# A retention layer and a wave MLP on one core: q loaded in 1024-byte rows, a half of the partitions at a time, in a new order of work

## The chip, the cores and the metric

One core of a Trainium2 chip runs the whole kernel. The metric is device time in microseconds (us) of one execution; the time given is the median of the runs. An engine is PE (matrix), DVE (vector), ACT (scalar) or POOL; SP only issues DMAs. ACT and POOL issue DMAs too.

## The reference

The inputs are q, k and v of shape (4, 8, 768, 64) (batch, head, token, dimension), and four weights. Cut to what matters:

```python
for t in range(S):                                   # retention, scale = 1/8
    state = gamma[h] * state + outer(k[t], v[t])     # gamma[h] = 1 - 2**(-5-h)
    y[t] = scale * q[t] @ state
x = y as (batch, token, 512)
theta = x @ w_theta
y = w_tok_r @ (x * cos(theta)) + w_tok_i @ (x * sin(theta))   # over tokens
u = x + y
out = u + maximum(u @ w_ch, 0)                       # float32 (4, 768, 512)
```

## The kernel before, in words

**Units and chunks.** The attention is cut into 24 units. Unit n is 256 tokens of four heads: n % 2 is the half of the heads, n // 2 the block of 256 tokens, three blocks to a batch. A chunk C is 128 tokens of all 512 columns, 24 in all, six to a batch. Two units (2i and 2i + 1) make chunks 2i and 2i + 1.

**The order is written out by hand.** `ORDER` is a list of tokens; each calls the function of its name with its arguments, and the last letter may name the engine or the queue (`a` ACT, `v` DVE, `p` POOL, `s` SP). Each engine and each queue works through its own tokens in that order. The steps:

| token | what it does | engine |
|---|---|---|
| Lq, Lk, Lv n | load q, k or v of unit n, 256 KB float32, two tokens to a partition, rows of 512 bytes | SP or ACT queue |
| ck, cq, cqs, cv n | cast k, cast q, or scale q by its decay, scale v; to bf16 (tiles kqb, vb) | letter |
| Tk, Tq, E n or Dk n | transpose k and q: on PE (tile kq_ps) with a copy E to kqT, or by a DMA transpose on SP | PE + letter, or SP |
| A, m n | k times q (at_ps), then the causal mask (at) | PE, DVE |
| ST, S0, S1, SB n | k times v, the state's running sum, its copy to bf16 (sbd) | PE, DVE or letter |
| I, Y n | state times q and at times v, into r_ps | PE |
| XA or XB n.c | r_ps to xT; XA multiplies by the decay table qx, XB copies where cqs scaled q already | DVE, letter |
| Tx, Ex C or Dx C | transpose xT to x, by PE and a copy or by a DMA transpose | PE + letter, or SP |
| Hh, CN C, z C | theta (th_ps), its sine and cosine, times x | PE, ACT, letter |
| Pth, Pch, Pw r.g | load w_theta (wth), w_ch (wch), a group of rows of w_tok_r or w_tok_i; float32 in HBM, cast to bf16 on the way | POOL queue |
| Tw, Ew r.t | transpose a block of w_tok | PE, letter |
| M t.s, u t | one of six token blocks of chunk t's y (y_ps), both weights; then u = x + y | PE, DVE |
| Tu, Eu t or Du t | transpose u, by PE and a copy or by a DMA transpose | PE + letter, or SP |
| O, f, SO t | u times w_ch (o_ps); maximum and sum (tile ot, 4 buffers); store of 256 KB | PE, DVE, SP or ACT queue |
| Mh, uh, Tuh, Euh, Oh, fh, SOh | the same for the last chunk in two column halves, with stores of 128 KB | as above |
| Z | two matmuls of zeros of 512 columns (tile zz) | PE |

The const tokens make tables: const1 zeros and tiles, const2 positions and log decays, const3 the decays qsc (for cqs) and vsc (for cv), constA positions along tokens, const8 and const9 the table qx for the first 256 and the other 512 tokens, const4 the identity, const5 the causal mask, const6 zeroes sbd, const7 a first sine.

M needs z of all six chunks of a batch, and so all six units of it.

Of the kernel before, what the change touches and what calls it, by code (L numbers as in the profile page):

```python
# [15 lines left out]
FT = mybir.dt.float32  # L16
# [6 lines left out]
const2 Lv.0.s const1 const6.v Z.29 Z.2 const5 Z.38 Lk.0.a const3 Z.35 Z.8 Lq.0.s Lv.1.s Z.28 constA  # L23
const4 Lq.1.a cqs.0.v const9 Lk.1.s cv.0.p Z.39 const8 ck.0.p Tk.0 Tq.0 ck.1.a E.0.v Lq.4.a ST.0
Lk.4.a Z.15 A.0 cqs.1.p Tq.1 Lq.2.s S0.0.v SB.0.1.v Lk.2.s SB.0.0.p cv.1.p Lv.2.s S1.0 I.0 Z.27 m.0
Tk.1 E.1.a Y.0 ST.1 XB.0.1.a cqs.2.v Z.34 S0.1.v S1.1 cv.2.p SB.1.0.a Pth Lq.3.s Z.18 XB.0.0.v Tq.2
A.1 SB.1.1.a ck.2.a Tk.2 const7 I.1 Z.23 m.1 Y.1 XB.1.0.a Lk.3.s E.2.v XB.1.1.v A.2 ck.3.p m.2 ST.2
# [54 lines left out]
M.22.0 M.21.5 M.22.3 M.22.5 Du.19 M.21.4 SO.17.s M.22.4 Du.18 M.21.0 O.19 Mh.1.0 Mh.1.2 M.21.3
M.20.2 Mh.1.4 u.22 O.18 f.19 M.20.0 M.20.1 Tuh.0 u.21 Du.22 Du.21 f.18 M.20.3 Euh.0 M.20.4 Mh.1.1
M.20.5 u.20 O.22 Mh.1.5 uh.1 f.22 Tu.20 SO.14.a SO.19.s Eu.20.a O.21 SO.18.a Tuh.1 Euh.1 f.21 O.20
f.20 Oh.0 Oh.1 SO.21.a SO.22.s SO.20.s fh.1 SOh.1 fh.0 SOh.0 Z.31
# [14 lines left out]
def kernel(  # L100
# [64 lines left out]

    def Lq(n, e):
        load_unit("qf", q, n, e)
# [35 lines left out]
    def const2():  # L203
        posn = const.tile([P, nI, 2], FT, name="posn")
# [9 lines left out]
        K["zerob"] = const.tile([P, 1], FT, name="zerob")  # L214
        nc.gpsimd.memset(K["zerob"], 0.0)
# [78 lines left out]
    def ck(n, e):  # L294
        copy(e, in_blocks(kqb_of(n)[:, 0]), by_token(raw["kf", n]))
# [338 lines left out]
```

## Time and profile before

| what | before |
|---|---|
| median of 3 runs | 169.24 us (168.81, 169.24, 169.62) |
| the profiled execution's own time | 168.7 us |
| its span | 166.9 us |
| busy: PE, DVE, ACT, POOL | 153.7, 114.0, 78.7, 76.6 us |
| DMA packets, bytes | 69,062, 34.93 MB |
| one load of q, from issue to landing, median | 5.0 us on SP's queue, 5.4 us on ACT's |

The span runs from the first to the last record of the profiled execution; the time of that execution lies 1.8 us above it. The page's slices cut the span into 40 equal parts of 4.17 us, and a digit is a busy share in tenths. The DMA share is the sum over the 16 DMA engines of the time that packets took; it can exceed 1 in the table of stretches, since packets of one engine overlap. Line numbers are those of the kernel before.

### The profile page before, as it was taken

What the parts mean: (1) busy time and instruction counts of PE and PEld (TensorE: products, weight loads), DVE (VectorE), ACT (ScalarE), POOL (GpSimd) and SP (SyncE); (2) the same over time, 40 slices, a digit from 0 to 9 for tenths busy, and PEclk for the clock granted to TensorE, in tenths of its full rate; (3) what the DMA queues carried; (4) which work ended last, traced back from release to release, by engine and by line L of the source; (5) the groups of instructions that cost most, each with busy time, mean ns of one, the idle gap of its engine ahead of it and who ended that gap; (6) DMA issues with size and microseconds to landing.
All of it is one profiled execution on the core that took longest, in us unless ns stands there. A gap on an engine that the chain in (4) does not pass through costs nothing.

```text
span 166.9 us, 4887 instructions
## 1 busy us (share of the span) xinstructions
PE 153.7 (92%) x2001; PEld 86.8 (52%) x2030; DVE 114.0 (68%) x210; ACT 78.7 (47%) x141; POOL 76.6 (46%) x110
## 2 busy tenths in 40 slices
PE   5997779998999999999999999969999999999992
PEld 2455546655666556654555555435545544454550
DVE  3298657989994896994779895659868561254462
ACT  4965879981558345763333735822151426000020
POOL 7957369179206642630217699910459303600000
PEclk9999999999999999999999999999999999999999
DMA  4999999999999998949999995999899539414355
GB/s 121 297 290 244 280 282 265 259 227 251 195 197 224 296 184 203 312 102 266 298 301 191 173 245 146 260 215 232 150 216 162 119 64 247 159 61 127 88 211 208
DMA packets 69062, 34.93 MB, mean 209 GB/s; under 512 B 26416, under 2 KB 66096, under 8 KB 69040
## 3 DMA queue, kind: packets, MB, share of 16 engines
q1 hardware_dynamic: 56032, 23.73, 66.9%
q10 hardware_dynamic: 10320, 7.47, 15.5%
q0 software_dynamic: 2688, 3.41, 12.1%
q8 instruction: 16, 0.26, 0.7%
q14 instruction: 6, 0.05, 0.1%
HBM read 25.69 MB, written 6.29 MB: 192 GB/s over the span
## 4 chain that ended last, share of the span: by engine, by line
PE 75%; DMA 11%; ACT 5%; DVE 4%; issue 2%; POOL 2%; DVEq 0%; SPq 0%; POOLq 0%; ACTq 0%
PE y_ps L509 34%; PE o_ps L536 11%; PE th_ps L469 10%; DMA kqf<-in_k_dram 4%; PE r_ps L423 4%; DMA kqf<-in_q_dram 3%; DMA out_dram<-ot 3%; ACT qx L233 3%; PE at_ps L346 3%; PE w_ps L491 3%; PE r_ps L411 2%; PE kq_ps L316 2%; PE y_ps L561 2%; PE x_ps L455 1%; PE r_ps L373 1%
## 5 line engine op out<-in xcount | busy, mean ns | idle before, releaser
L509 PE MATMUL y_ps<-z,wtr 128*128 128x512 bf16 x131 | 49.8, 380 | 2.2 <-DVE ot L542 1.2
L509 PE MATMUL y_ps<-z,wti 128*128 128x512 bf16 x131 | 49.7, 379 | 1.0 <-issue 1.0
L483 POOL TENSOR_TENSOR z<-cs,x_sb 128x1024 bf16<-128x1024 bf16 x12 | 25.4, 2122 | 17.6 <-ACT cs L476 9.8
L355 DVE TENSOR_TENSOR at<-at_ps,mask 128x1024 bf16<-128x1024 f32 x24 | 29.2, 1216 | 0.6 <-PE at_ps L346 0.5
L308 POOL TENSOR_TENSOR vb<-vf,vsc 128x512 bf16<-128x512 f32 x18 | 18.8, 1047 | 21.3 <-DMA vf<-in_v_dram 20.9
L542 DVE SCALAR_TENSOR_TENSOR ot<-o_ps,u 128x512 f32<-128x512 f32 x23 | 15.9, 689 | 15.3 <-PE o_ps L536 12.1
L469 PE MATMUL th_ps<-wth,xT 128*128 128x512 bf16 x88 | 23.9, 380 | 0.5
L516 DVE TENSOR_TENSOR u<-y_ps,x_sb 128x512 bf16<-128x512 f32 x23 | 15.8, 688 | 11.5 <-PE y_ps L509 11.3
L536 PE MATMUL o_ps<-wch,uT 128*128 128x512 bf16 x88 | 23.2, 380 | 0.4 <-issue 0.2
L476 ACT ACTIVATE cs<-th_ps,zerob 128x512 bf16<-128x512 f32 x24 | 16.4, 685 | 13.0 <-PE th_ps L469 8.5
L476 ACT ACTIVATE cs<-th_ps,halfpi 128x512 bf16<-128x512 f32 x24 | 16.3, 685 | 12.9 <-issue 6.8
L139 POOL CAST sbd<-s 64x256 bf16<-64x256 f32 (+1 forms) x21 | 8.9, 423 | 26.9 <-DVE s L391 24.8
L509 PEld LDWEIGHTS <-wti 128*128 128x128 bf16 x138 | 13.5, 98 | 14.2 <-issue 2.5
L509 PEld LDWEIGHTS <-wtr 128*128 128x128 bf16 x138 | 13.4, 97 | 12.8
L137 ACT COPY kqT<-kq_ps 128x1024 bf16<-128x1024 bf16 x11 | 11.1, 1012 | 8.7 <-PE kq_ps L316 8.7
L137 ACT CAST kqb<-kqf 128x512 bf16<-128x512 f32 x17 | 10.3, 619 | 7.7 <-DMA kqf<-in_k_dram 6.0
L469 PEld LDWEIGHTS <-xT 128*128 128x128 bf16 x96 | 8.8, 98 | 8.3
L536 PEld LDWEIGHTS <-uT 128*128 128x128 bf16 x92 | 8.4, 98 | 8.6
L316 PE MATMUL kq_ps<-ident,kqb 128*128 128x128 bf16 x120 | 11.0, 220 | 0.5 <-ACT kqb L137 0.2
L278 PE MATMUL zz<-zero 128*128 128x512 bf16 x27 | 9.3, 477 | 2.0 <-DVE zero L192 1.9
L137 ACT CAST sbd<-s 64x256 bf16<-64x256 f32 (+1 forms) x19 | 6.9, 363 | 8.7 <-DVE s L139 4.0
L423 PE MATMUL r_ps<-at,vb 64*64 64x128 bf16 x384 | 10.0, 221 | 1.0 <-DVE at L355 1.0
(77 smaller groups left out, 207.0 us busy)
## 6 DMA issues: line engine op xcount, KB each, us to landing
vf<-in_v_dram SPq DMA_DIRECT2D x20, 256.0 KB, 5.8
kqf<-in_k_dram SPq DMA_DIRECT2D x19, 256.0 KB, 5.2
kqf<-in_q_dram SPq DMA_DIRECT2D x17, 256.0 KB, 5.0
out_dram<-ot ACTq DMA_DIRECT2D x12, 256.0 KB, 2.9
out_dram<-ot SPq DMA_DIRECT2D x11, 256.0 KB, 3.1
kqf<-in_q_dram ACTq DMA_DIRECT2D x7, 256.0 KB, 5.4
kqf<-in_k_dram ACTq DMA_DIRECT2D x5, 256.0 KB, 4.8
vf<-in_v_dram ACTq DMA_DIRECT2D x4, 256.0 KB, 5.3
```

The costliest lines, as they stand in the source:

```text
L137: nc.scalar.copy(dst, src)
L308: engines[e].tensor_mul(in_blocks(vb), by_token(raw["vf", n]), _bcast_last(K["vsc"][:, i, :, h * HU:(h + 1) * HU], D))
L316: nc.tensor.transpose(st["kq_ps", n][:, 4 * w + x, :], st["kqb", n][:, w, x * P:(x + 1) * P], K["ident"])
L355: nc.vector.tensor_mul(at.rearrange("p g j a t -> p (g j) (a t)"), st["at_ps", n].rearrange("p g j a t -> p (g j) (a t)"), _bcast_mid(K["m ...
L423: nc.tensor.matmul(st["R", n + 1][c][g * D:(g + 1) * D, j * P:(j + 1) * P], st["vb", n][rows, lo:lo + D], st["at", n][rows, g, j, a, :], s ...
L469: nc.tensor.matmul(th_ps, st["xT", C][:, j, :], K["wth"][:, j, :], start=(j == 0), stop=(j == 3))
L476: nc.scalar.activation(st["cs", C][:, w, :], st["th_ps", C], AF.Sin, bias=K["zerob" if w else "halfpi"], scale=1.0)
L483: engines[e].tensor_mul(st["z", b][:, c], st["cs", C], _bcast_mid(x_of(C), 2))
L509: nc.tensor.matmul(st["y", t], K["wT"][r][:, s0, t0 * P:(t0 + 1) * P], st["z", b][:, s0, r, :], start=(done == 0 and r == 0), stop=(done = ...
L516: nc.vector.tensor_add(st["u", t], st["y", t], st["x", b][:, t0, :])
L536: nc.tensor.matmul(o_ps, st["uT", t][:, j, :], K["wch"][:, j, :], start=(j == 0), stop=(j == nD - 1))
L542: nc.vector.scalar_tensor_tensor(st["ot", t], st["o", t], 0.0, st["u", t], ALU.max, ALU.add)
```

## The change

q is loaded by two DMAs a unit, Lq (partitions 0 to 63) and Lr (64 to 127), each 128 KB. A partition now holds four tokens of two heads in place of two tokens of four heads, so that a row in HBM is 1024 bytes. Everything that reads q follows: the scale table qsc has four tokens and two heads to a partition, cq and cqs put four token groups of 128 columns into kqb, A and I take 4 x 32 columns of the transposed q in place of 2 x 64, the mask and XA and XB have four tokens in place of two. k and v stay as they are. The table qx, which XA uses, is kept.

const2 now begins with the zero bias and a first Exp on ACT, and makes positions and log decays for q's new layout (two more position fills on POOL, eight small fills and one product on DVE).

The order is new throughout. In numbers of tokens: q loads 24 to 48 (Lq and Lr); loads issued by ACT 16 to 36 and by SP 56 to 60; Dk 9 to 10, Dx 12 to 11, Du 16 to 17; z on POOL 12 to 8; XB on ACT 17 to 10 and on DVE 9 to 16; Ew on ACT 3 to 8; SB on ACT 19 to 24; cv on POOL 18 to 15; Z 15 to 13. XA stays at 22, and M, Hh, O, A, Y, I and ST stay as they are in number.

```diff
+    def q_load(n, j, e):
+        b, i, h = unit(n)
+        if ("qf", n) not in raw:
+            raw["qf", n] = io.tile([P, 2, 4, D], FT, name="kqf", bufs=16)
+        queues[e].dma_start(
+            out=raw["qf", n][j * D:(j + 1) * D].rearrange("p g a d -> p g (a d)"),
+            in_=q[b, h * HU:(h + 1) * HU, i * 2 * P:(i + 1) * 2 * P, :].rearrange(
+                "(j g) (p a) d -> j p g (a d)", g=2, a=4)[j])
     def Lq(n, e):
-        load_unit("qf", q, n, e)
+        q_load(n, 0, e)
+    def Lr(n, e):
+        q_load(n, 1, e)
...
     def const2():
+        K["zerob"] = const.tile([P, 1], FT, name="zerob")
+        nc.gpsimd.memset(K["zerob"], 0.0)
+        nc.scalar.activation(const.tile([P, 1], FT, name="warm"), K["zerob"], AF.Exp,
+                             bias=K["zerob"], scale=1.0)
...
+    def q_by_token(ap):
+        return ap.rearrange("p g a d -> p a g d")
+    def q_blocks(ap):
+        return ap.rearrange("p (a g d) -> p a g d", a=4, g=2)
+    def qT(n, rows, j, c):
+        lo = j * D + c * D // 2
+        return st["kqT", n][rows, 1].rearrange("p a j t -> p (a j) t")[:, :, lo:lo + D // 2]
...
     def cq(n, e):
-        copy(e, in_blocks(kqb_of(n)[:, 1]), by_token(raw["qf", n]))
+        copy(e, q_blocks(kqb_of(n)[:, 1]), q_by_token(raw["qf", n]))
...
-                                         kqT[rows, 1, :, j, cols],
+                                         qT(n, rows, j, c),
...
-        return (st["xT", C][:, 2 * h:2 * h + 2].rearrange("p j (t a) -> p j t a", a=2),
-                st["R", n + 1][c][:, :2 * P].rearrange("p (j a t) -> p j t a", j=2, a=2))
+        return (st["xT", C][:, 2 * h:2 * h + 2].rearrange("p j (t a) -> p j t a", a=4),
+                st["R", n + 1][c][:, :2 * P].rearrange("p (j a t) -> p j t a", j=2, a=4))
```

The order up to the first M, before and after:

```text
before
const2 Lv.0.s const1 const6.v Z.29 Z.2 const5 Z.38 Lk.0.a const3 Z.35 Z.8 Lq.0.s Lv.1.s Z.28 constA
const4 Lq.1.a cqs.0.v const9 Lk.1.s cv.0.p Z.39 const8 ck.0.p Tk.0 Tq.0 ck.1.a E.0.v Lq.4.a ST.0
Lk.4.a Z.15 A.0 cqs.1.p Tq.1 Lq.2.s S0.0.v SB.0.1.v Lk.2.s SB.0.0.p cv.1.p Lv.2.s S1.0 I.0 Z.27 m.0
Tk.1 E.1.a Y.0 ST.1 XB.0.1.a cqs.2.v Z.34 S0.1.v S1.1 cv.2.p SB.1.0.a Pth Lq.3.s Z.18 XB.0.0.v Tq.2
A.1 SB.1.1.a ck.2.a Tk.2 const7 I.1 Z.23 m.1 Y.1 XB.1.0.a Lk.3.s E.2.v XB.1.1.v A.2 ck.3.p m.2 ST.2
S0.2.v S1.2 SB.2.1.a Z.11 cqs.3.p Tq.3 Lv.3.s Tx.0 Tk.3 Z.3 ck.4.p Lv.4.s Lk.5.s Lq.5.s Lv.5.s
Lq.6.s Lk.6.s Lv.6.s Lq.7.s E.3.a SB.2.0.v I.2 Y.2 XB.2.1.a Ex.0.a cv.3.v cq.4.p Tk.4 Lq.8.s A.3
ST.3 Lk.7.s S0.3.v SB.3.0.a S1.3 Lv.7.s Lk.8.s Tx.1 Tq.4 SB.3.1.p cv.4.p m.3 Pw.1.0 XB.2.0.a Ex.1.a
I.3 Lv.8.s cq.5.a Y.3 E.4.a Pw.0.0 ST.4 Hh.0 ck.5.a cv.5.v CN.0.1 A.4 CN.0.0 S0.4.v Tq.5 Hh.1 Tk.5
XB.3.0.v SB.4.0.p XB.3.1.v SB.4.1.a Pw.0.1 Hh.2 m.4 E.5.v I.4 Y.4 ST.5 ck.6.a Tk.6 Tx.2 cq.6.a
CN.1.1 CN.1.0 XA.4.1 A.5 XA.4.0 m.5 Lq.9.s Ex.2.v S0.5.v z.0.p Tq.6 E.6.a CN.2.0 cv.6.p Hh.3
SB.5.0.v Tx.3 Tw.1.0 z.1.v SB.5.1.a Ew.1.0.v Ex.3.a CN.2.1 A.6 I.5 Y.5 ST.6 XA.5.0 z.2.v Tw.0.0
CN.3.0 Tx.4 CN.3.1 Ew.0.0.v S0.6.v XA.5.1 Ex.4.v Hh.4 CN.4.0 CN.4.1 Tw.0.1 M.0.1
...
M.20.5 u.20 O.22 Mh.1.5 uh.1 f.22 Tu.20 SO.14.a SO.19.s Eu.20.a O.21 SO.18.a Tuh.1 Euh.1 f.21 O.20
f.20 Oh.0 Oh.1 SO.21.a SO.22.s SO.20.s fh.1 SOh.1 fh.0 SOh.0 Z.31

after
const1 Z.40 Z.2 Z.10 const2 constA const4 Lv.0.a Lr.0.s Lr.1.s Lq.1.s Lq.0.a const5 const6.v const3
const8 Lk.0.s cq.0.a cq.1.a Z.43 Z.25 Lk.1.s ck.1.a cv.0.v ck.0.v ST.0 S0.0.v S1.0 Lk.2.s Lk.4.s
Tk.0 Tq.0 SB.0.1.a E.0.v Tk.1 Lv.1.s Lr.2.s ck.4.p cv.1.p ck.2.a SB.0.0.a I.0 A.0 Lq.2.s Lk.3.a Tq.1
Lq.3.s cqs.2.p Lr.4.s Z.18 Tk.2 Lq.4.s Lv.2.s E.1.a m.0 const9 Lr.3.a Z.37 Y.0 cq.3.a A.1 cqs.4.v
Tq.2 Tk.4 Z.17 ck.3.a Z.7 XA.0.0 E.2.v ST.1 cv.2.p Pth m.1 Lv.4.s Lk.5.s S0.1.v Lq.5.s SB.1.0.p
cv.4.p XA.0.1 A.2 S1.1 Tq.3 Tk.3 SB.1.1.a Lv.3.s I.1 Y.1 ST.2 Lr.5.s Lr.6.s m.2 XA.1.0 E.3.a Z.20
S0.2.v cq.5.a SB.2.1.a Lr.7.a Pw.0.0 S1.2 Tq.4 Tx.0 A.3 XA.1.1 Pw.0.1 Z.39 Lq.6.s SB.2.0.p I.2 E.4.a
cv.3.p Pw.1.0 cq.6.p Y.2 ST.3 Ex.0.v m.3 ck.5.a S0.3.v S1.3 XB.2.1.a A.4 SB.3.0.p Lv.5.s XB.2.0.v
Tx.1 Tq.5 SB.3.1.a Tk.5 Z.27 Lk.6.s Lv.6.s E.5.v I.3 Y.3 ST.4 XA.3.1 Z.0 XA.3.0 S0.4.v Tx.3 const7
cv.5.p SB.4.0.p Ex.3.a SB.4.1.a Lr.8.a Hh.0 Hh.1 Tx.2 Ex.1.v m.4 I.4 Y.4 ST.5 A.5 Tq.6 CN.0.1 Lk.7.a
CN.0.0 CN.1.1 CN.1.0 Ex.2.v Lk.8.a Lv.7.a z.0.v XB.4.1.a Hh.3 Tw.0.0 XB.4.0.v ck.6.p z.1.v Pw.1.1
S0.5.v SB.5.1.p Tk.6 Hh.2 CN.3.1 SB.5.0.p m.5 Ew.0.0.v Lq.8.a E.6.a I.5 Y.5 XA.5.1 Lv.9.a A.6 CN.3.0
Tw.0.2 CN.2.1 cv.6.p z.3.v Ew.0.2.a CN.2.0 Tw.1.0 Lr.9.a Hh.5 Ew.1.0.v Pw.1.2 CN.5.1 Pch XA.5.0
z.2.v Tw.0.1 Tx.5 Hh.4 ST.6 CN.5.0 Lq.7.s Ex.5.v z.5.v Ew.0.1.a Lv.8.s CN.4.0 CN.4.1 S0.6.a SB.6.1.p
Tx.4 M.0.0
...
M.20.3 M.20.2 Tuh.1 SO.18.a Euh.0 Euh.1 u.20 SO.15.s SO.19.s Du.22 O.22 Du.21 f.22 Tu.20 Eu.20.a
Oh.0 Oh.1 fh.0 fh.1 SO.22.a SOh.0 O.20 f.20 O.21 SO.20.s f.21 SO.21.s SOh.1
```

In the middle of the new order SO.7.s stands just ahead of A.19, M.12.1, M.12.2, M.12.5 and O.11, and f.11 behind them.

More of the change, by code (lines that the diff above doesn't have):

```diff
@@ L22 @@
 ORDER = """
[L23 to L27, printed above, removed]
@@ L82 @@
[L82 to L85, printed above, removed]
+const1 Z.40 Z.2 Z.10 const2 constA const4 Lv.0.a Lr.0.s Lr.1.s Lq.1.s Lq.0.a const5 const6.v const3
+const8 Lk.0.s cq.0.a cq.1.a Z.43 Z.25 Lk.1.s ck.1.a cv.0.v ck.0.v ST.0 S0.0.v S1.0 Lk.2.s Lk.4.s
@@ new lines @@
+Tk.0 Tq.0 SB.0.1.a E.0.v Tk.1 Lv.1.s Lr.2.s ck.4.p cv.1.p ck.2.a SB.0.0.a I.0 A.0 Lq.2.s Lk.3.a Tq.1
+Lq.3.s cqs.2.p Lr.4.s Z.18 Tk.2 Lq.4.s Lv.2.s E.1.a m.0 const9 Lr.3.a Z.37 Y.0 cq.3.a A.1 cqs.4.v
+Tq.2 Tk.4 Z.17 ck.3.a Z.7 XA.0.0 E.2.v ST.1 cv.2.p Pth m.1 Lv.4.s Lk.5.s S0.1.v Lq.5.s SB.1.0.p
+cv.4.p XA.0.1 A.2 S1.1 Tq.3 Tk.3 SB.1.1.a Lv.3.s I.1 Y.1 ST.2 Lr.5.s Lr.6.s m.2 XA.1.0 E.3.a Z.20
+S0.2.v cq.5.a SB.2.1.a Lr.7.a Pw.0.0 S1.2 Tq.4 Tx.0 A.3 XA.1.1 Pw.0.1 Z.39 Lq.6.s SB.2.0.p I.2 E.4.a
+cv.3.p Pw.1.0 cq.6.p Y.2 ST.3 Ex.0.v m.3 ck.5.a S0.3.v S1.3 XB.2.1.a A.4 SB.3.0.p Lv.5.s XB.2.0.v
@@ new lines @@
+z.2.v Tw.0.1 Tx.5 Hh.4 ST.6 CN.5.0 Lq.7.s Ex.5.v z.5.v Ew.0.1.a Lv.8.s CN.4.0 CN.4.1 S0.6.a SB.6.1.p
+Tx.4 M.0.0 M.0.2 Ex.4.v cqs.7.v z.4.v M.0.1 Tw.1.1 Pw.0.2 cv.7.p S1.6 ck.7.p M.0.5 cqs.8.p M.0.3
+M.0.4 Ew.1.1.a u.0 m.6 M.1.5 M.1.2 Lq.9.s Lk.9.s SB.6.0.a M.1.4 M.1.1 I.6 Tw.1.2 Ew.1.2.v Tk.7 Tq.7
+M.1.0 ck.8.a cv.8.v Tk.8 M.1.3 E.7.a Y.6 ST.7 XA.6.1 S0.7.v XA.6.0 A.7 m.7 S1.7 SB.7.0.p Tu.0 M.2.5
+M.2.1 Tq.8 SB.7.1.a Eu.0.a E.8.a M.2.4 M.2.3 Tw.1.4 Lr.11.s Lq.12.s Ew.1.4.a Lq.11.s I.7 M.2.0 A.8
@@ new lines @@
+Tq.15 f.5 cv.15.v Y.13 ST.14 M.8.1 M.8.4 Lv.20.s Lr.17.s u.9 XA.13.0 XA.13.1 cqs.16.v S0.14.v
+SB.14.0.p M.8.0 M.8.5 M.8.3 S1.14 Hh.13 E.15.a SO.3.a Lq.19.s Eu.6.a M.8.2 SB.14.1.v cv.20.v I.14
+Y.14 A.15 ST.15 Du.7 Lq.17.s u.8 XA.14.0 S0.15.v Lv.19.a CN.13.0 CN.13.1 Lk.19.a M.10.5 O.6 M.10.3
+S1.15 f.6 m.15 XA.14.1 cv.16.v SB.15.1.a ck.19.v M.10.4 M.10.2 Dk.18 Lk.21.a SB.15.0.p cqs.17.p
+cv.17.p cqs.19.p Hh.12 CN.12.1 Tx.13 M.10.0 M.10.1 Dk.16 Lr.21.a CN.12.0 Lv.18.s Ex.13.a I.15 Y.15
+ST.16 z.13.p A.16 O.7 u.10 Tx.12 Dk.17 XA.15.1 S0.16.v XA.15.0 f.7 Hh.15 M.11.5 Ex.12.a ck.20.a
@@ L213, in const2 @@
         nc.gpsimd.memset(K["halfpi"], math.pi / 2.0)
-        K["zerob"] = const.tile([P, 1], FT, name="zerob")
-        nc.gpsimd.memset(K["zerob"], 0.0)
+        posq = const.tile([P, nI, 4], FT, name="posq")
+        lgq = const.tile([P, 2, 2], FT, name="lgq")
+        for j in range(2):
+            rows = slice(j * D, (j + 1) * D)
+            nc.gpsimd.iota(posq[rows], pattern=[[2 * P, nI], [1, 4]], base=1, channel_multiplier=4,
+                           allow_small_or_imprecise_dtypes=True)
+            for h in range(2):
+                for g in range(2):
+                    nc.vector.memset(lgq[rows, h, g:g + 1], math.log(gammas[h * HU + 2 * j + g]))
+        argq = const.tile([P, nI * 4, 4], FT, name="argq")
+        nc.vector.tensor_mul(argq, _bcast_last(posq.rearrange("p i a -> p (i a)"), 4),
+                             _bcast_mid(lgq.rearrange("p h g -> p (h g)"), nI * 4))
+        K["argq"] = argq
         arg = const.tile([P, nI * 2, H], FT, name="arg")
@@ L266, in const5 @@
                     out=mask[rows, a], in_=mask[rows, a], compare_op=ALU.is_ge, fill=0.0,
-                    base=-a, pattern=[[1, 2], [2, D]], channel_multiplier=-2)
+                    base=-a, pattern=[[1, 4], [4, D // 2]], channel_multiplier=-2)
         K["mask"] = mask
```

118 lines of the change are left out of this document (55 added, 63 removed).

## The prediction

> **What bounds the kernel now.** I read the page first: the busy rows and the slices.
>
> ```profile
> PE 153.7 (92%) x2001; PEld 86.8 (52%) x2030; DVE 114.0 (68%) x210; ACT 78.7 (47%) x141; POOL 76.6 (46%) x110
> ...
> PE   5997779998999999999999999969999999999992
> ...
> DMA  4999999999999998949999995999899539414355
> ```
>
> PE is busy 92% of the span and the only engine near it; its weak slices are the first eight (to 33 us) and one at 109 us. DMA is full up to about 115 us. So there are two stages: one in which PE waits for data, and one in which it has a stock of work. The chain of waits over the first 30 us shows where they join.
>
> ```profile
> 9.25 6.63 DMA kqf<-in_k_dram
> ...
> 15.90 0.37 SPq L157
> ...
> 16.31 5.65 DMA kqf<-in_q_dram
> ...
> 22.04 0.62 ACT kqb L137
> 22.66 0.92 ACT kqT L137
> 23.59 0.04 issue
> 23.63 0.42 PE at_ps L346 x16
> ```
>
> Everything up to A.4 (23.63) hangs on two loads: k of unit 4 lands at 15.88, and only then SP issues Lk.5.s; q of unit 5 lands at 21.97, ACT does cq.5, then E.4, then PE does A.4. From there the chain is PE. The stretches tell how fast data comes, what outputs cost, and where PE still has holes.
>
> ```profile
> 6.00:9.00 3.00, 2.79 (x39) 1.25 (x41) 1.69 (x3) 3.00 (x7) 2.41 (x3) 1.00 1.22 290
> ...
> 108.00:111.00 3.00, 2.01 (x53) 1.01 (x53) 0.44 (x1) 1.44 (x4) 0.90 (x3) 1.00 1.34 202
> ...
> 162.00:164.00 2.00, 1.78 (x12) 0.97 (x10) 1.53 (x4) 0.00 (x0) 0.00 (x0) 1.00 0.83 303
> ```
>
> The columns are the stretch, its length, busy time of PE, PEld, DVE, ACT and POOL, PE's clock, the DMA share and GB/s. Loads in 512-byte rows move 290 GB/s at a share of 1.22, so 256 KB takes 0.90 us. The first two loads land near 5.1 us, and at 0.90 us each the fourteenth should land at 5.1 + 12 x 0.90 = 15.9: it does (15.88). The seventeenth (q of unit 5) should land at 18.6 and lands at 21.97; the 3.4 us between are wth, issued by POOL at 12.51: 1.05 MB of float32 at 290 GB/s is 3.6 us. The start is therefore bound by bytes. From 30 us to PE's last useful matmul (163.3) the stretches of 6 us leave PE idle only 4.5 us, 1.24 of it in the second row above, where DVE's f.11 waits for an output store:
>
> ```profile
> 110.56 0.69 DVE L542 SCALAR_TENSOR_TENSOR ot<-o_ps,u 128x512 f32<-128x512 f32 x1 [3.05 <-DMA out_dram<-ot]
> ```
>
> The end is 163.3 (last Oh), two halves of fh to 164.08, and a 128 KB store issued at 164.10; span 166.9, profiled run 168.7, so 1.8 us lie around the span. The median shown is 169.24, 0.54 above that run.
>
> **The change part by part.**
>
> *q's packets.* Six q units must land before A.4 in both orders, and 17 unit loads in all (v 0-4, k 0-5, q 0-5). A unit of q goes from 512 packets of 512 bytes to 256 of 1024. Upper end of the gain: outputs (2 KB rows) move 303 GB/s at share 0.83, 365 per unit of share against 290/1.22 = 238, so at equal share 256 KB takes 0.59 us. A straight line per packet between 1.77 ns (0.90 us / 512) and 4.6 ns (0.59 us / 128) gives 2.7 ns at 1024 bytes, 0.70 us a unit: 0.20 saved. Other end: no load of before writes only 64 partitions; if a half got half the rate, a unit would take 1.80 us, 0.90 lost. Size is nearest to the load rows, and the two changes pull apart, so I take a saving of 0.10 a unit, 0.6 us by A.4; ends -1.2 and +5.4.
>
> *POOL's weight loads.* Pth moves behind cv.2.p, that is behind v of unit 2, which has 12.5 units up to and with it: 5.1 + 10.5 x 0.90 = 14.5, plus 1.04 for cv.2: issue at 15.6 instead of 12.51. So part of wth falls behind q of unit 5. But Pw.0.0 and Pw.0.1 (0.39 and 0.79 MB of float32) follow cv.4.p on the same queue, near 17 instead of 21.9 and 24.2. With 1.05 MB landing 6.9 us after issue the POOL queue gets half to 0.6 of the rate; q of unit 5 then lands at L = 18.0 + 0.5 (L - 15.6) = 20.4, or 21.6 with 0.6 (the 0.6 us of q is in the 18.0). Against 21.97 that is -0.4 to -1.6 for both items; I take **-1.0**.
>
> *ACT ahead of A.4.* SB.2.1.a (0.40) and the issue Lr.7.a now stand between cq.5.a and E.4.a: **+0.4**. Nothing hides it, E.4 is what A.4 waits for.
>
> *PE's stock at A.4.* Before, PE has done Hh.0 (0.86), ST.4 (0.29), I.3 (0.22), Y.3 (0.35) and Tx.1 (0.22) ahead of A.4; after, they come behind: 1.94. Taken away are one unit's Tk and Tq (8 transposes, 0.44) and a Tu (0.22), each to a DMA transpose, and one Tx more (0.22): -0.44. Sum 1.5; the rows overlap a little (the work behind A.4 sums to 138.7, PE took 135.2), so **+1.4**.
>
> *Zero matmuls.* Z.27 and Z.0 (0.86 each) now stand behind A.4; before had none there. Where PE would wait anyway they are free, where it would not they cost 1.7. I take half, **+0.85**. Z.31 at the end hung on nothing: 0.
>
> *The end.* The last steps on PE become Oh.0 Oh.1 O.20 O.21; then f.21 (0.69) instead of two fh (0.76), and a 256 KB store (3.1 from issue to landing on SP) instead of 128 KB (1.8), partly under the end's idle DMA: 0.2 to 1.3, taken **+0.6**. Du.21 has 5.2 us of PE work to hide in and needs about 4.8.
>
> *What costs nothing.* const9 (2.9 us on ACT) leaves the front and const8 stays; from 9.25 on the chain is loads at full rate, so ck.1 gains and A.4 doesn't. The earlier table load lies under the first loads. Without that cover: 2.9. cqs.4.v now stands ahead of XA.0.0, E.2.v and m.1 on DVE and waits for q of unit 4 (11.5 units: 13.7), so m.1 starts near 15.5 instead of 12.91, and Y.1 with it; hidden as long as units 1 to 3 are through when q of unit 5 lands; else about +1. 24 more load DMAs, and loads on ACT's queue grow from 16 to 36 at 0.44 us: SP's ninth load (Lq.2.s, 5.14) waited for the first to land, and Lk.5.s for k of unit 4, eight DMAs ahead of it, so eight seem to be the most in flight. Eight now hold about 1.5 MB instead of 2, 5.4 us at 290 GB/s against a landing of 5.2: just enough, but a load stuck behind ACT's work holds SP's eighth after it. 0, or up to 2 late. POOL loses 12 us (z 12 to 8 at 2.12, fewer vb), DVE gains 2, ACT 5; none is the bound. f.11's store SO.7.s has about 2.5 us of PE work ahead of f.11 against 2.9 to 6.1 to landing: that hole stays. The patterns with four tokens keep all shapes: 0.
>
> Sum: -1.0 + 0.4 + 1.4 + 0.85 + 0.6 = +2.25 on 168.7, 171.0; plus 0.54 to the median: 171.5, rounded to **171.4**.
>
> **The rivals.**
> *The halves are served badly.* If a half is slowed to half the rate and a third of that is not covered by other loads on the second queue, a q unit costs 0.30 more: by A.4 +1.8 instead of -0.6, 2.4 above the forecast: 173.8, more if the 18 later units slow the full DMA stage. For: DMA is full to 115 us. Against: two queues run.
> [...]
> *Faster, by the weight load.* Place: the POOL queue around 15.6 us. If the sixteen engines serve q, k and v first and leave nearly all of wth (3.4 us) for after q of unit 5, A.4 comes 3.4 + 0.6 - 1.0 = 3.0 earlier than in my sum and, with Hh.0 still fed in time, the end is 168.4. If the two Z lie in waits as well, 167.5. It decides once more than about 2.6 us of wth moves behind q, with Z free. For: Pth really moves; against: Pw moves forward, and wth landed no slower than the loads around it.
> *No difference.* Z free and q's full gain: 171.4 - 0.85 - 0.6 = 169.95, close to 169.24 with one hole less in the middle. That the rows don't really become 1024 bytes is excluded by the access pattern.
>
> **How the numbers follow.** Forecast (170.2 to 172.8) 0.43, halves served badly 0.20, no difference 0.13, faster 0.24. About 0.5% (0.85 us) is what a measurement of this kernel can tell from no change. Faster 0.24, same 0.13, slower 0.63. The range takes the faster case's 167.5 and most of the bad halves: 167.5 to 174.2.
>
> **What would show it.** About 63,600 packets instead of 69,062 (6,144 fewer for q, some 700 more for one more DMA transpose); GB/s of the early slices above 297 (packets win) or below 280 (halves lose); the chain with q of unit 5 landing near 21.0 and A.4 near 23.0; zz matmuls after it without idle before them; the last store 256 KB. Wrong if A.4 starts before 21 or after 25, if PE's idle time after 35 us is under 3 or over 7, or if the chain in the middle runs through DMAs.

## The result and the profile after

The changed kernel takes **177.13 us** (median of 4 runs, 176.13 to 178.62) where the kernel before, run beside it, takes 169.43: a ratio of 1.0479, 95% interval 1.0434 to 1.0524. Slower was forecast (171.4), but the time lies above the whole range (167.5 to 174.2). The profiled execution is the slowest of the four: 178.62 us, span 176.9; its mean granted clock is 0.949, the others' 0.96 to 0.99. In all that follows medians are over all runs of a kernel, while the ratios, by which the comparisons go, leave out the runs in a slower state of the chip, and the profiles of e1, e5, e11 and e12 are of such runs.

The page of the changed kernel, the rows that answer to those shown of before: busy times, the slices of PE, its granted clock, the DMA share, the GB/s, the packets, and the shares of the chain that ended last.

```profile
PE 160.9 (91%) x2018; PEld 88.6 (50%) x2018; DVE 114.7 (65%) x221; ACT 83.1 (47%) x149; POOL 65.6 (37%) x102
...
PE   7487699999999999999999899999499999999991
...
PEclk9957669999999999999999999999969999999998
DMA  5999999999999999998999999699992736633625
GB/s 123 272 250 268 229 216 239 209 246 240 241 222 254 213 219 208 268 236 192 260 237 247 203 276 162 165 222 215 166 202 99 113 63 161 165 89 89 207 78 193
DMA packets 64358, 35.19 MB, mean 199 GB/s; under 512 B 27856, under 2 KB 61392, under 8 KB 64336
...
PE 55%; DMA 25%; DVE 5%; SPq 4%; ACT 4%; POOL 3%; issue 3%; ACTq 0%; DVEq 0%; POOLq 0%
```

The page of before, the same two rows, GB/s and the chain:

```profile
GB/s 121 297 290 244 280 282 265 259 227 251 195 197 224 296 184 203 312 102 266 298 301 191 173 245 146 260 215 232 150 216 162 119 64 247 159 61 127 88 211 208
...
PE 75%; DMA 11%; ACT 5%; DVE 4%; issue 2%; POOL 2%; DVEq 0%; SPq 0%; POOLq 0%; ACTq 0%
```

The DMA row is as full as before over the first 120 us, yet the early slices move 272, 250, 268, 229 and 216 GB/s; before moved 297, 290, 244, 280 and 282. There are fewer packets and fewer bytes a microsecond at the same share. The chain is 25% DMA; it was 11% before. Two stretches of the changed kernel:

```profile
6.00:9.00 3.00, 1.04 (x26) 0.83 (x27) 1.22 (x4) 1.73 (x4) 0.05 (x1) 0.93 1.20 281
...
20.00:28.00 8.00, 7.75 (x138) 5.13 (x136) 4.44 (x10) 5.11 (x10) 4.61 (x7) 0.65 1.19 220
```

The second stretch of before:

```profile
20.00:28.00 8.00, 6.39 (x134) 4.17 (x136) 5.05 (x10) 6.49 (x12) 5.84 (x7) 1.00 1.18 282
```

From 6 to 9 us nearly as many bytes move as before (281 against 290 GB/s), but PE works 1.04 us in place of 2.79. From 20 to 28 us the DMA engines are as full as before and move 220 GB/s in place of 282, and PE's clock is 0.65.

The chain of waits up to A.4, start and length of each piece:

```profile
11.54 1.01 ACT kqT L138
12.55 0.35 ACT qx L261
12.90 5.95 DMA kqf<-in_q_dram
...
18.87 0.63 ACT kqb L138
...
19.55 1.13 PE kq_ps L355 x8
```

A.4 in PE's timeline:

```profile
25.86 0.39 PE L385 MATMUL at_ps<-kqT 64*64 64x128 bf16 x16
```

The load on it is the upper half of q of unit 3 (Lr.3.a). ACT issues it only at 12.90, behind E.1 and the start of const9; it needs 5.95 us to land, and cq.3 waits for it. A.4 stands at 25.86; before it was 23.63. Further on, loads of k and q (50.79, 58.15, 69.02, 92.94 us; 5.2 to 7.5 us each) are pieces of the chain, which before held no load there, only one store. The longest hole in PE's later part is now 2.64 us:

```profile
127.57 1.44 PE L575 MATMUL o_ps<-wch,uT 128*128 128x512 bf16 x4 [2.64 <-ACT cs L515]
```

### The profile page after: what moved, and what is told of

Its sections match the earlier page's. It is cut to its first block, busy times and chain, and to the rows that moved or that the text cites. A ratio compares the mean times of both kernels' runs of the same rounds, so it can differ in the third digit from the quotient of the medians.

```text
span 176.9 us, 4961 instructions
## 1 busy us (share of the span) xinstructions
PE 160.9 (91%) x2018; PEld 88.6 (50%) x2018; DVE 114.7 (65%) x221; ACT 83.1 (47%) x149; POOL 65.6 (37%) x102
## 2 busy tenths in 40 slices
DMA packets 64358, 35.19 MB, mean 199 GB/s; under 512 B 27856, under 2 KB 61392, under 8 KB 64336
## 4 chain that ended last, share of the span: by engine, by line
PE 55%; DMA 25%; DVE 5%; SPq 4%; ACT 4%; POOL 3%; issue 3%; ACTq 0%; DVEq 0%; POOLq 0%
PE y_ps L548 25%; DMA kqf<-in_k_dram 14%; PE th_ps L508 7%; PE o_ps L575 6%; DMA kqf<-in_q_dram 6%; PE r_ps L462 3%; DMA out_dram<-ot 3%; DMA x_sb<-xT 2%; PE kq_ps L355 2%; PE r_ps L450 2%; PE at_ps L385 2%; SPq L171 2%; PE y_ps L600 1%; PE zz L307 1%; PE r_ps L412 1%
## 5 line engine op out<-in xcount | busy, mean ns | idle before, releaser
L548 PE MATMUL y_ps<-z,wtr 128*128 128x512 bf16 x138 | 52.5, 381 | 0.6 <-DVE z L522 0.5
L548 PE MATMUL y_ps<-z,wti 128*128 128x512 bf16 x138 | 52.3, 379 | 0.0
L575 PE MATMUL o_ps<-wch,uT 128*128 128x512 bf16 x92 | 24.4, 395 | 3.1 <-ACT cs L515 2.6
L522 POOL TENSOR_TENSOR z<-cs,x_sb 128x1024 bf16<-128x1024 bf16 x8 | 17.0, 2130 | 12.4 <-ACT cs L515 8.0
L140 POOL CAST sbd<-s 64x256 bf16<-64x256 f32 (+1 forms) x17 | 6.8, 401 | 37.8 <-DVE s L430 28.1
L347 POOL TENSOR_TENSOR vb<-vf,vsc 128x512 bf16<-128x512 f32 x15 | 15.6, 1040 | 10.1 <-DMA vf<-in_v_dram 9.5
L138 ACT CAST sbd<-s 64x256 bf16<-64x256 f32 (+1 forms) x24 | 8.7, 362 | 13.9 <-DVE s L430 12.3
L140 POOL CAST kqb<-kqf 128x512 bf16<-128x512 f32 x11 | 7.2, 654 | 16.6 <-DMA kqf<-in_k_dram 15.0
L341 POOL TENSOR_TENSOR kqb<-kqf,qsc 128x512 bf16<-128x512 f32 x9 | 9.4, 1048 | 10.4 <-PE y_ps L548 8.5
L522 DVE TENSOR_TENSOR z<-cs,x_sb 128x1024 bf16<-128x1024 bf16 x16 | 11.5, 716 | 2.4 <-DMA x_sb<-xT 1.1
```

What stands on the lines that cost most here:

```text
L138: nc.scalar.copy(dst, src)
L140: engines[e].tensor_copy(dst, src)
L341: engines[e].tensor_mul(q_blocks(kqb_of(n)[:, 1]), q_by_token(raw["qf", n]), _bcast_last(K["qsc"][:, i, :, h], D))
L347: engines[e].tensor_mul(in_blocks(vb), by_token(raw["vf", n]), _bcast_last(K["vsc"][:, i, :, h * HU:(h + 1) * HU], D))
L522: engines[e].tensor_mul(st["z", b][:, c], st["cs", C], _bcast_mid(x_of(C), 2))
L548: nc.tensor.matmul(st["y", t], K["wT"][r][:, s0, t0 * P:(t0 + 1) * P], st["z", b][:, s0, r, :], start=(done == 0 and r == 0), stop=(done = ...
```

## The experiments

In the diffs, a line `ORDER` stands for the list of tokens.

### The order alone, and the load alone

**e1**, the new order with q's old load:

```diff
 kernel before
-ORDER (before)
+ORDER (after), zerob and the first Exp as after
+    def Lr(n, e): pass
```

> The new order, with q loaded as before (one DMA a unit, 128 partitions, 512-byte rows; Lr does nothing). Before 169.4, after 177.1. Theory H (a DMA to half of the partitions moves slower, and the slow loads starve PE): most of the 7.7 us goes away, 169 to 172, and the early slices come back from 216-272 to 245-297 GB/s. Theory O (the new order itself): stays at 175 to 178. Theory N (the number of DMAs, each of which takes one of about eight places in flight): 169 to 172 like H, since 24 DMAs go.

Measured: 172.04 us, ratio 1.0126 (1.0083 to 1.0170). The new order costs 2.1 us by the ratio, 2.8 by the medians. So some 6 of the 8 us lie in how q is loaded.

**e2**, the old order with the new load, both halves issued by Lq:

```diff
 kernel after
-ORDER (after)
+ORDER (before)
     def Lq(n, e):
         q_load(n, 0, e)
+        q_load(n, 1, e)
```

> The old order with the new layout and the new loads (Lq issues both halves one behind the other on the queue that the old order names). H: slower by 3 to 8 us, 172 to 177, early GB/s down to about 230-260. O: 168 to 170. N: slower too, 171 to 176.

Measured: 180.05 us, ratio 1.0609 (1.0523 to 1.0695). The new load costs more in the old order (6.1%) than in the new one (4.8 less e1's 1.3).

**e3, e4, e6 and e8** vary the load in the old order.

```diff
 e3: kernel before, two loads of q, 64 partitions each, rows of 512 bytes
+        for j in range(2): ... out=t[j * D:(j + 1) * D] ... in_= tokens j * P to (j + 1) * P
 e4: kernel before, two loads of q, all partitions, two heads each, rows of 512 bytes
+        for j in range(2): ... out=t[:, 2 * j:2 * j + 2] ... in_= heads 2 * j to 2 * j + 2
 e6: kernel after with the ORDER of before, one load of q, all partitions, rows of 1024 bytes
+        out=t, in_=q[b, h * HU:h * HU + 2, t0:t0 + 4 * P, :] (512 tokens of two heads)
 e8: kernel before, one load of 512 KB for q of two units; k and q buffers 9 and 4
```

> The kernel before, q by two DMAs of 64 partitions each with the old 512-byte rows and layout. H: the slowest of the four, 174 to 180, as the halves bring no longer rows. O: 169 to 170. N: 171 to 176, the same as two DMAs of 128 partitions with two heads each.

> The kernel before, q by two DMAs of 128 partitions each, two heads to a DMA, 512-byte rows: as many DMAs and bytes as in the halves, but all partitions. H: 169 to 170.5, GB/s as before. O: 169 to 170. N: 171 to 176, as slow as the halves.

> The old order with the new layout in all the steps behind the load, and q by one DMA of 128 partitions in 1024-byte rows. It brings the wrong tokens (two heads of 512 tokens instead of four of 256), so the output is not the reference's; bytes, DMA count and all other work are those of the kernel before. If the layout and the longer rows cost nothing: 167.5 to 169.5. If the steps with four tokens are dearer, or the longer rows are slower: 171 to 174, since the old order with halves of 1024-byte rows measured 180.1 against 176.9 with 512-byte rows.

> The kernel before with q of both units of a block (all eight heads) in one DMA of 512 KB, issued at the first of the two Lq tokens: 12 DMAs fewer; 4 such tiles and 9 for k in place of 16 shared. If the number of DMAs in the window is a price in the kernel before too: 166.5 to 168.5. If only halves cost: 168.5 to 170. Less depth for k could cost up to 2 us.

Measured: e3 176.94 us (ratio 1.0438, 1.0361 to 1.0514); e4 173.16 (1.0223, 1.0142 to 1.0303); e6 168.82 (0.9953, 0.9928 to 0.9979), with q of other tokens; e8 170.36 (1.0053, 1.0024 to 1.0082). In the old order, then, two loads in place of one cost 2.2%, the cut into halves costs 2.1% more, and rows of 1024 bytes on all partitions gain 0.5%. Fewer, larger loads (e8) gain nothing. Halves in rows of 1024 bytes (e2, 6.1%) are dearer here than halves in rows of 512 (e3, 4.4%); why was not taken apart. The stretches 4 to 12 and 12 to 20 us of e3:

```profile
4.00:12.00 8.00, 6.49 (x97) 3.42 (x96) 3.84 (x7) 6.19 (x10) 5.12 (x13) 1.00 0.94 206
12.00:20.00 8.00, 4.08 (x82) 2.14 (x82) 5.05 (x11) 3.90 (x9) 3.09 (x4) 0.92 1.07 198
```

The same stretches of before:

```profile
4.00:12.00 8.00, 7.51 (x99) 3.89 (x99) 4.30 (x9) 6.77 (x12) 5.88 (x14) 1.00 1.21 294
12.00:20.00 8.00, 6.47 (x156) 4.57 (x157) 6.01 (x13) 5.79 (x12) 4.62 (x7) 1.00 1.20 261
```

e4 moved 260 and 187 at shares of 1.01 and 0.96, so much of it comes with the number alone: in e3 and e4, where a unit's two loads follow each other on one queue, the share falls from 1.2 to below 1.1, and the DMA engines are less busy.

### The new order with other loads

**e5, e10, e13, e9 and e16** keep the new order and change q's load only.

```diff
 e5: e1, Lq and Lr each two heads, all partitions, rows of 512 bytes
+        out=raw["qf", n][:, 2 * j:2 * j + 2], in_= heads 2 * j to 2 * j + 2
 e10: kernel after, one load (Lq), all partitions, rows of 1024 bytes; Lr empty
+        out=t, in_=q[b, h * HU:h * HU + 2, t0:t0 + 4 * P, :]
 e13: kernel after, two loads, all partitions, rows of 1024 bytes
+        out=raw["qf", n][:, j], in_=q[b, h * HU + j, t0:t0 + 4 * P, :] as "(p a) d -> p (a d)"
 e9: kernel after, two loads, all partitions, cut by heads in place of halves
-            out=raw["qf", n][j * D:(j + 1) * D], in_= ... "(j g) (p a) d -> j p g (a d)"[j]
+            out=raw["qf", n][:, j], in_= ... "(j g) (p a) d -> g j p (a d)"[j]
 e16: kernel after, two loads, even and odd partitions
-            out=raw["qf", n][j * D:(j + 1) * D]
+            out=raw["qf", n][j::2]
```

> The new order with both loads of a unit kept at their places (Lq and Lr), but each over all 128 partitions: two heads, 512-byte rows, the old layout. The same number of DMAs and bytes as after. The new order with one load a unit measured 172.0, after 177.1. Theory H (half of the partitions is what costs): near 172 to 173.5. Theory N (24 more DMAs in a window of eight): 175 to 177. Both matter about equally if it lands at 174 to 175.

Measured: 172.79 us, ratio 1.0110 (1.0051 to 1.0169). With as many loads as the changed kernel, over all partitions, the new order is no slower than with one load a unit.

> The changed kernel with q loaded by one DMA a unit (Lq, 128 partitions, 1024-byte rows), Lr issues nothing; the DMA reads 512 tokens of two heads in place of 256 of four, so q holds other tokens than the reference needs. Theory: 170.5 to 172, as the new order with q's old load (172.0) or up to 1.5 below it, by the rows; so the order alone accounts for 2 to 3 us over before. If the number of loads counts in the new order too, it is 1 us or more below the run with two loads over all partitions; if not, the same within 0.7.

Measured: 171.72 us, ratio 1.0123 (1.0092 to 1.0155). Beside e1 (1.0126), the longer rows gain nothing in the new order.

> The changed kernel with its layout, order, two loads of 128 KB a unit and rows of 1024 bytes; each load fills all 128 partitions with one head of 512 tokens, so q holds other tokens than the reference needs. If 64 partitions are the cause: 171.5 to 173 us, about 5 below the changed kernel, near the 171.7 of one load a unit and the 172.8 of two loads with 512-byte rows. If the number of loads and their places are the cause: 175 to 177.5.

Measured: 171.37 us, ratio 1.0165 (1.0117 to 1.0214): 3.1% or 5.3 us below the changed kernel, with the same order, rows, sizes, queues and number of loads (64,357 packets against 64,358). Beside e10 the number of loads makes no difference that the intervals show. The page of e13, GB/s and chain:

```profile
GB/s 165 301 316 309 252 233 243 285 263 235 241 257 216 201 298 266 158 179 276 318 173 278 209 202 192 111 303 160 176 172 158 112 46 183 127 93 93 216 94 184
...
PE 70%; DMA 14%; DVE 6%; ACT 2%; issue 2%; SPq 2%; ACTq 0%; POOL 0%; DVEq 0%
```

Slices 2 to 4 are back above 300, and DMA's share of the chain is 14%, with no load of q, k or v in it behind 16.43 us. This is the main result: what costs is that each load fills one half of the partitions. Whether it is the number, 64, or where they lie, e16 asks.

> The changed kernel whole, its layout of q, its order, its two loads of 128 KB a unit in 1024-byte rows, correct values; only the cut between the two loads differs: Lq brings the first head of each pair to all 128 partitions, Lr the second, in place of one half of the partitions each. Theory (the halves of the partitions are what was mis-sized): 170.5 to 173 us, some 5 us below the changed kernel's 177.1, since the same order with halved loads of 512-byte rows over all partitions took 172.8; early stretches at 260 to 290 GB/s; A.4 near 22 to 23.5. Rival (the number of loads, the order or ACT's queue make the loss, and halves only add to it): 175 to 178. If the rows bring what the streams showed (0.75 against 0.90 us for 256 KB), 171 rather than 172.8.

Measured: 282.97 us, ratio 1.6716 (1.6657 to 1.6774): neither theory. The packets of e9 say why.

```profile
DMA packets 63686, 35.19 MB, mean 125 GB/s; under 512 B 27184, under 2 KB 60720, under 8 KB 63664
```

There are 672 small packets fewer than in the changed kernel (27,184 against 27,856), 14 for each of the 48 loads. Elsewhere a further load brings 16 (384 more in e13 than in e10, for 24 loads). Read as one small packet for each DMA engine that a load uses, 2 of 16 engines carried each in e9. The DMA share fits: from 6.0 to 7.5 us, with PE, DVE, ACT and POOL idle, it is 0.14 at 45 GB/s, and 2 of 16 is 0.125. In HBM the slowest dimension of e9's pattern is j, of size 2, the same number; no other size was run, so it is not shown that the size sets the number.

> The changed kernel, order, sizes, rows and queues; only Lq fills the even partitions and Lr the odd ones, in place of the lower and the upper half, so rows of q lie in other partitions than the steps behind take them from. If neighbouring partitions are the cause: 171 to 173 us, as the run with two loads over all 128 partitions (171.4); early stretches at 280 to 310 GB/s. If it is 64 partitions a load, whichever they are, or the longer issue: 175.5 to 178.

Measured: 173.16 us, ratio 1.0212 (1.0172 to 1.0252). 2.7% (of the time of the kernel before) come back when the 64 partitions of a load are every other one, with the longer issue and all else kept; the 0.5% left to e13 is within what the intervals leave open. The rate says the same (slices 2 to 4 move 294, 315 and 305):

```profile
GB/s 126 294 315 305 237 231 281 240 283 233 237 262 241 208 264 270 164 194 265 290 245 239 213 142 188 103 264 190 262 103 172 107 81 182 76 101 105 221 140 108
```

### Loads by themselves

**e7 and e15** load and compute nothing: phases of 24 units of 256 KB, the mix being k on SP, v on ACT, q on SP in turn.

> Loads alone, no matmuls; the output is zeros but for one column. Ten phases of 24 loads of 256 KB (6.29 MB), DVE reads the tiles between phases. Phases: 1 one DMA of 128 partitions, 512-byte rows, on SP; 2 two DMAs of two heads each; 3 two DMAs of 64 partitions, 512-byte rows; 4 the same with 1024-byte rows; 5 one DMA of 128 partitions, 1024-byte rows; 6 like 4, lower half from SP and upper half from ACT; 7 like 1, SP and ACT in turn; 8, 9, 10 k from SP, v from ACT and q from SP as in 1, 4 and 5. H: phases 3 and 4 run at 170 to 230 GB/s against 280 to 300 in phase 1 and 300 to 350 in phase 5; phase 6 comes back to over 250; phase 9 lies 5 to 15% under 8. N: phase 2 falls as far as phase 3, because fewer bytes are in flight. If neither: all phases within 10% of phase 1, and the loss is in the kernel's waits.

Stretches of three phases of e7, q on SP's queue: one load a unit in 512-byte rows, two halves in 1024-byte rows, one load in 1024-byte rows. The last two columns are the DMA share and GB/s.

```profile
4.00:24.00 20.00, 0.92 (x6) 0.00 (x0) 1.00 1.16 285
92.00:118.00 26.00, 0.77 (x5) 0.00 (x0) 1.00 0.68 200
125.00:140.00 15.00, 0.57 (x4) 0.00 (x0) 1.00 1.06 341
```

> Loads alone, in eleven phases of 24 units of 256 KB, with nothing computed. Phases 1 to 5 are q on SP's queue in 1024-byte rows: 1 two DMAs over 128 partitions, 2 two halves of the partitions (200 GB/s in the earlier run), 3 every other partition, 4 the lower half only, 5 one DMA of 256 KB on 64 partitions, lower and upper in turn. Phases 6 to 11 are the mix k on SP, v on ACT, q on SP: 6 q as before (290 GB/s earlier), 7 halves (252), 8 two DMAs over 128 partitions, 9 every other partition, 10 256 KB on 64 partitions, 11 halves on two queues. If 64 partitions limit a DMA: phase 1 at 260 to 310, phases 2 to 5 near 200, 4 below 2. If bytes in flight limit: 1 and 2 alike near 200 to 250, 5 at 290. If only neighbouring partitions matter: 3 like 1. Mix: 8 at 280 to 300, and 9 to 11 between 250 and 290 tell the same.

One stretch of each phase of e15, in their order:

```profile
5.00:24.00 19.00, 1.40 (x10) 0.00 (x0) 1.00 0.89 268
31.00:58.00 27.00, 1.54 (x10) 0.00 (x0) 1.00 0.66 196
66.00:92.00 26.00, 1.40 (x10) 0.00 (x0) 1.00 0.66 200
100.00:126.00 26.00, 0.95 (x10) 0.00 (x0) 1.00 0.72 197
134.00:152.00 18.00, 0.00 (x0) 0.00 (x0) 1.00 1.14 218
165.00:181.00 16.00, 0.61 (x4) 0.00 (x0) 1.00 1.20 293
190.00:208.00 18.00, 0.31 (x2) 0.00 (x0) 1.00 1.19 255
217.00:233.00 16.00, 0.62 (x4) 0.00 (x0) 1.00 1.16 310
241.00:257.00 16.00, 0.61 (x4) 0.00 (x0) 1.00 1.16 308
265.00:281.00 16.00, 0.61 (x4) 0.00 (x0) 1.00 1.19 249
290.00:310.00 20.00, 0.43 (x5) 0.00 (x0) 1.00 1.13 251
```

Two different limits show. Phases 2 to 4 (lower and upper half, every other partition, lower half only) have shares near 0.7: the engines are not full. SP issued the 48 loads of each in 31.5 to 31.9 us, 0.66 us a load, against 0.47 in phase 1; I read that as a limit of the issuing queue, since it is the same for all three and halves on two queues moved 262 GB/s alone (e7). Phase 5 has half as many issues, a full share of 1.14, and still only 218 GB/s against 341 over all partitions. That limit is not the queue's. In the mix, which is what the kernel does, the issue is hidden: halves move 255 GB/s (249 in one load, 251 by two queues), every other partition 308, all partitions 310. So it is not how many partitions, how many bytes or which queue, but where the 64 lie. Every set tried was a half or every other partition, so the runs don't tell neighbours from partitions of one half (32 to 95 were not tried). What makes the place count (255 against 308) is not shown.

### Other steps of the forecast, and two misses

**e11** and **e12** start from e1.

```diff
 e11: ORDER, Z.27 and Z.0 taken out
 e12: ORDER
-cqs.2.p Lr.4.s ... cv.2.p Pth m.1
+cqs.2.p Pth Lr.4.s ... cv.2.p m.1
```

> The new order with q's old load (172.0 us in its own run), and the two zero tokens behind A.4, Z.27 and Z.0, taken out. By the forecast's term they cost 0.85: 171.2. If PE waits there anyway (the changed kernel showed PE waiting 2.2 us behind the first of them), 172.0, no difference; if PE's clock falls without them, slower.

Measured: 171.27 us, ratio 1.0090 (1.0064 to 1.0116) against e1's 1.0126: 0.6 us less, but the intervals overlap. It fits a price of 0.85 and does not exclude none.

> The new order with q's old load (172.0 us), and the load of w_theta (Pth) issued by POOL right behind cqs.2.p, near 12.5 us, in place of behind cv.2.p, 15.9 us: where it stood in time before. By the forecast moving it late saved about 0.4 us up to A.4, so here A.4 comes 0.4 later, near 22.9 instead of 22.5, and the end 172.0 to 172.4. Rival: Hh.0 and Hh.1 wait for w_theta in the new order (it lands at 25.4), so bringing it early gives 0.5 to 1.5 us: 170.5 to 171.5.

Measured: 174.90 us, ratio 1.0186 (1.0129 to 1.0243) against e1's 1.0126: 1 us more, but the intervals overlap. A.4 in the timelines of e1 and of e12, one line each:

```profile
21.18 0.41 PE L352 MATMUL at_ps<-kqT 64*64 64x128 bf16 x16
```

```profile
23.42 0.67 PE L352 MATMUL at_ps<-kqT 64*64 64x128 bf16 x16
```

In these two profiles A.4 is 2.2 us later with w_theta early: in e12's chain a load of v needs 9.75 us (6.52 in e1). The sign is the forecast's, the size more than five times its 0.4; it rests on one profile each. The rival of this run (that Hh waits for w_theta) is seen in e1, with 0.68 us of PE, and is the smaller effect.

**e14**, the two halves on two queues:

```diff
     def Lq(n, e):
         q_load(n, 0, e)
+        q_load(n, 1, "a" if e == "s" else "s")
-    def Lr(n, e): q_load(n, 1, e)
+    def Lr(n, e): pass
```

> The changed kernel, but Lq issues both halves, the lower on its own queue and the upper on the other one (SP and ACT), at the place of Lq; Lr issues nothing. With loads alone the two halves on two queues moved 262 GB/s against 200 on one. If one queue for both halves is the cause, 173 to 175. If 64 partitions cost in any mix, 176 to 179, and more if ACT's queue now holds SP's loads up.

Measured: 193.00 us, ratio 1.1344 (1.1296 to 1.1392): above both ranges. The edit does more than it names: the half that Lr issued moves to Lq's place, and ACT's queue issues 24 loads of q in place of 18. In the chain of e14 one load of q spans the time from 23.31, when ACT gets to issue it, to its landing, and PE stands idle from 28 to 31 us:

```profile
23.31 7.61 DMA kqf<-in_q_dram
```

So e14 points to loads held up behind ACT's work, which was not tested by itself, and says nothing of two queues; phase 11 of e15 does (251 against 255).

**e17**, eight more zero tokens where PE is idle ahead of A.4:

```diff
 ORDER
-cv.0.v ck.0.v ST.0 ... XA.0.1 A.2 S1.1 Tq.3
+cv.0.v ck.0.v Z.50 Z.51 Z.52 Z.53 ST.0 ... XA.0.1 Z.54 Z.55 A.2 S1.1 Z.56 Z.57 Tq.3
```

> The changed kernel and eight more zero tokens on PE: four ahead of ST.0 (idle 5.5 to 7.7 us), two ahead of A.2 and two ahead of Tq.3 (idle 1.2 us each). If the low clock costs time of its own: granted clock 1.00 at 20 to 24 us, and about 4.5 us of PE work that ran at half rate ahead of A.4 takes 2 less, so 174.5 to 176 us. If the loads alone set when A.4 comes: 176.5 to 177.5, whatever the clock. If the zero tokens are in the way: above 177.5.

Measured: 178.54 us, ratio 1.0489 (1.0415 to 1.0563), against 1.0479 without them. The clock's row of e17:

```profile
PEclk9978999999999999999999999999999999999999
```

The slices from 17 us on are at full clock now (the changed kernel had 6 and 6 in tenths there), and the time is the same. The profiles say why only in part. From the landing of Lr.3 to A.4 the changed kernel takes 7.0 us (18.85 to 25.86), e17 5.4 (21.03 to 26.41): PE is faster by 1.6, but the load lands 2.2 later. So a higher clock gained nothing in the whole time; that the low clock costs nothing where the load comes in time is not shown.

## Why the prediction missed

**The term that failed is "q's packets".** It weighed 0.20 gained by the rows against 0.90 lost by the halves and took a saving of 0.10 a unit, "nearest to the load rows". In e15's mix three units (k, v, q; 786 KB) take 786/293 = 2.68 us with q as before and 786/255 = 3.08 with halves: a loss of **0.40 a unit**. Over all partitions the same rows and number of loads give 786/310 = 2.54, a gain of 0.15. So the price of the rows was about right for loads alone (in the kernels they gain 0.5% in the old order and nothing in the new one), and the other end was the one to take. The rival "The halves are served badly" had the mechanism and the sign; its own size (0.30 a unit) was near. It failed in its reach: it counted six units by A.4 and put the 18 later ones into a clause without a number, so 173.8 stood where 24 x 0.50 = 12 us were at stake (0.40 lost instead of 0.10 gained), as far as loads bind. DMA full to 115 us, read from the page of before, was the sign that they do. From e13 to the changed kernel the whole grows by 5.3 us by the ratios, or 0.22 a unit. In the two profiles, 7.3 us apart, A.4 comes 4.05 later (21.81 to 25.86): Lr.3 is issued 1.2 later (12.90 for 11.69), needs 1.2 longer (5.95 for 4.74), and from its landing to A.4 pass 7.0 in place of 5.4, with PE's clock at 0.50 from 20 to 24 us (e17, at full clock there, needs 5.4 too). The other 3.2 lie behind A.4, where loads are pieces of the changed kernel's chain (50.79 to 92.94) and of e13's none.

**POOL's weight loads**: the place and the sign held; issue of wth was forecast at 15.6 and is 15.92 in e1. The size did not: with q's old load (e1) A.4 is at 21.18, where the sum without the packets keeps it at 23.63; e12 points the same way. The rival *Faster, by the weight load* was thus right up to A.4: with one load of 1024-byte rows (e10) A.4 is at 20.14, 3.5 us ahead of before, and wth lands at 22.1, behind q of unit 5, which is cast at 17.61. ACT ahead of A.4 (+0.4) has no run of its own.

**The terms behind A.4** (+1.4, +0.85) were too small. From A.4 to PE's end before took 139.7 us; e10 takes 146.1 and e13 144.1. So the order's sum (+2.85 without the packets: -0.4 + 0.4 + 1.4 + 0.85 + 0.6) meets e1's +2.1 to +2.8 only because two errors cancel. The zero matmuls were sized wrongly too: Hh.0, four matmuls of 512 columns, is priced at 0.86, so a Z, which is two, takes 0.43 at that rate and not 0.86, and +0.85 is the whole of both and not the half. (The sum itself gives 171.5; 171.4 is no rounding of it.) One piece of the longer stretch is f.11's hole, which was said to stay: 1.24 us of PE before (the row shown holds 0.99 of it), 2.86 in e10, whose DVE waits 4.43 us for the store:

```profile
124.97 0.69 DVE L588 SCALAR_TENSOR_TENSOR ot<-o_ps,u 128x512 f32<-128x512 f32 x1 [4.43 <-DMA out_dram<-ot]
```

In the changed kernel that place is another wait: ACT issues Lr.23 at 126.15, and CN.19's second half behind it starts at 126.83. What makes up the rest was not taken apart; it stays open.

**The end** cost 0.1, not 0.6: from PE's last matmul to the span's end 3.7 us against 3.6. **More loads** cost nothing that the intervals show in the new order, as forecast (e10, e13), but 2.2% in the old one (e4). They and the 20 more on ACT's queue were counted as "0, or up to 2 late"; the chain above shows one such load (12.90).

**What was to show it** spoke plainly. Early slices below 280 GB/s were named as "halves lose": 216 to 272 (slices 2 to 4 tell it, 250 to 272; slices 5 to 7 of e13, 233 to 252, lie below 280 too). A.4 after 25 (25.86) and a chain that runs through DMAs in the middle were named as wrong, and both came. PE's idle time after 35 us is 5.2 us, inside its bounds (3 to 7). Packets are 64,358, not 63,600: q's rows took off exactly 6,144 (e6: 62,918), but the order adds 1,055 (e10) where 700 were counted, and 24 more loads add 16 each, 384.

## What to carry to other kernels

A load to the lower or upper 64 partitions is slow even when other queues fill the DMA engines (255 GB/s in the mix against 310), and a DMA row that looks full hides it (a share of 1.19 with halves, 1.16 with all partitions): read GB/s beside the share. Price such a unit over the whole stage in which DMA is full, not only up to the first wait. A layout that needs two loads should deal them to every other partition (308), or to all partitions with a split inside them (310); the one pattern tried with an outermost dimension of 2 took 283 us (e9).

## What the runs showed that was not expected

Every other partition is as good as all of them in the mix (308 against 310 GB/s), while one load of 256 KB to 64 neighbours shows a full share (1.14) at 218 GB/s. A load to 64 partitions takes ACT's queue 0.62 us to issue (0.62 with every other partition too), one of as many bytes to all partitions 0.35 (medians of the changed kernel, e16 and e13). The pattern of e9, whose slowest dimension is 2, used, by my reading of the count of packets, 2 of 16 DMA engines and made the kernel 1.67 times as long as before. Raising the clock ahead of A.4, from 20 to 24 us, from 0.50 to 1.00 gained nothing in the whole time (178.54 us in e17 against 177.13).
